# A transposed residual, weight DMAs alone on SyncE's queue, and a layernorm of more steps, in a recurrent attention kernel

## The chip, the cores and the metric

The kernel runs on one core of a Trainium2 chip. The metric is the device time of one execution in microseconds (us). The core has five engines that run their own instruction streams: TensorE (PE; its weight loads are listed as PEld), VectorE (DVE), ScalarE (ACT), GpSimd (POOL) and SyncE (SP). SyncE and ScalarE issue the DMAs of this kernel, each from its own stream and in its order (SPq and ACTq in the profile); the transfers run on 16 DMA engines that both share.

## The reference

`x` is 2048 tokens of 1024 features. `xn` is its layernorm. The result is `x + A(xn) + B(xn)`.

```python
def _A_ref(x, mem0, Wq, Wk, Wv, Wo, seg_len):
    mem = mem0
    for s in range(n_seg):
        xs = x[:, s * seg_len:(s + 1) * seg_len, :].copy()
        h = jnp.concatenate([mem, xs], axis=1)
        q = jnp.einsum('btd,dhe->bhte', h, Wq)
        k = jnp.einsum('btd,dhe->bhte', h, Wk)
        v = jnp.einsum('btd,dhe->bhte', h, Wv)
        scores = jnp.einsum('bhqe,bhke->bhqk', q, k) * scale
        ...
        o = jnp.einsum('bhqk,bhke->bhqe', p, v)
        o = jnp.einsum('bhte,hed->btd', o, Wo)
        mem = o[:, :M, :].copy()
        outs.append(o[:, M:, :])
    return jnp.concatenate(outs, axis=1)
```

A is attention with a memory: 64 segments of 32 tokens, each with 8 memory tokens in front, 32 heads of 128. The memory of a segment is the output of the segment before, so the segments follow one another. The four weights are 8 MB each in bfloat16. B scores all tokens with a vector `w_r`, takes the two best, sends them through a gated MLP of width 3584, scales the result by the sigmoid of the score and adds it to these two tokens; all others pass as they are. So the output is `x + xn` (with two rows changed), plus `xn` of B, plus attention; the kernel calls the first part the residual.

## The kernel before

**Weights.** The four attention weights are cut into 64 granules of 128 x 2048 (512 KB): numbers 0 to 47 are the six phases of Q, K and V (`PHASES`, two halves of each, 8 granules a phase), 48 to 63 are Wo. 42 granules stay on the chip (`wres`, loaded once by `load_resident`, lines 103 to 109); the other 22, spread evenly, are streamed again in every segment (`granule`, lines 319 to 324) through the four slots of the pool `wstream` (tiles named g). A load into a slot waits until TensorE has read what was in it, four streamed granules before.

**Prologue.** For 16 tiles of 128 tokens: load x (`load_x`), statistics (`ln_a`), normalise (`ln_b`), transpose on TensorE and score with w_r (`ln_c`), and write three things to DRAM (`ln_d`, lines 217 to 221): `xT_d`, the transposed xn by segment; `stl_d`, the last 8 tokens of each of four segments, transposed; and `xr_d`, x + xn, row by row. The loop of lines 227 to 236 runs these steps for neighbouring tiles; each step of VectorE, ScalarE and TensorE is issued in the program's order. `rounded` (lines 156 to 161) sends small values through bfloat16 and back with two copies. Then comes B (the MoE stage, lines 243 to 312): the two best tokens, 46 granules of its weights through the same four slots, and the two new rows written into `xr_d`.

**A segment** (lines 371 to 586). The 24 first tokens of the segment and the 8 memory tokens make 32 columns of ST, the stationary operand; a granule is the moving one, in four column groups of the array. The other 8 tokens of each segment ("left") fill the 32 columns of STL for four segments at once: with G, j = divmod(s, 4), left V is done in the segment j = 0 (tile PSl, line 493), left Q and K of the next group at j = 1 and 2 (written to DRAM by line 415 and read back as QL and KL), and left Wo at j = 3 (tile WL). After each Q or K phase ScalarE casts the sums (XB, line 500) and TensorE transposes them one granule later; `hook(p, kc, fn)` puts scores and attention behind given granules. Phase Wo (lines 523 to 563) starts from the residual: one matmul of an identity with RT, 24 rows of `xr_d` per 256 columns, and at j = 3 another with RL. At its end WO is cast to OB, written out by four DMAs of ScalarE (line 568), transposed and copied into the next ST (lines 352 to 357, the copy of line 356 is the hand-over to the next segment). At j = 3 some left Wo work follows, then OL is written out by sixteen DMAs of ScalarE (line 581).

**Order.** The schedule is manual: every engine gets its instructions in the order in which Python issues them. SyncE's queue holds all loads. Between the last granule of V and the first of Wo stand, for the next segment, QL and KL (line 347), ST (328), four RT (339), at j = 0 STL (333), and at j = 3 sixteen RL (532). SyncE runs ahead of TensorE as far as the four slots let it, and waits in place for whatever its next DMA needs. STL is one buffer and is loaded again when TensorE has finished left V. The DMAs of SyncE and ScalarE together take eight completion semaphores in turn, in the program's order; a DMA waits until the one eight before it has landed, whichever engine issued it.

Of the kernel before, what the change touches and what calls it, by code (L numbers as in the profile page):

```python
# [18 lines left out]
N_SLOT = 4  # L19
# [6 lines left out]
def kernel(  # L26
# [67 lines left out]
    xT_d = [dram.tile([4, P, KC * SEG], BF16, name=f"xT_d{t}") for t in range(NT)]  # L94
    stl_d = [dram.tile([P, KC * SEG], BF16, name=f"stl_d{t}") for t in range(NT)]
    ql_d = [dram.tile([2, P, 4, P], BF16, name=f"ql_d{t}") for t in range(NT)]
    kl_d = [dram.tile([2, P, 4, P], BF16, name=f"kl_d{t}") for t in range(NT)]
    xr_d = dram.tile([S, D], BF16, name="xr_d")
# [15 lines left out]
    RT = [const.tile([P, 256], BF16, name=f"RT{i}") for i in range(2)]  # L114
    PL = [const.tile([P, 4, 2, 32], BF16, name=f"PL{i}") for i in range(2)]
    for i in range(2):
        nc.gpsimd.memset(RT[i][:, :], 0.0)
        nc.gpsimd.memset(PL[i][:, :, :, :], 0.0)
# [10 lines left out]
    for jq in range(4):  # L129
        q0 = 32 * jq  # L130
        nc.gpsimd.affine_select(out=MF[q0:q0 + 32, 0:NK], in_=MF[q0:q0 + 32, 0:NK], pattern=[[-1, NK]],
                                compare_op=ALU.is_ge, fill=NEG, base=0, channel_multiplier=1)
        nc.gpsimd.affine_select(out=MF[q0:q0 + 32, NK:2 * NK], in_=MF[q0:q0 + 32, NK:2 * NK], pattern=[[-1, NK]],
                                compare_op=ALU.is_ge, fill=NEG, base=SEG, channel_multiplier=1)
    for jq in range(4):
        nc.vector.memset(MF[32 * jq:32 * jq + M, 0:NK], 0.0)
    nc.vector.tensor_copy(out=MASK[:, :], in_=MF[:, :])

    XT = {}
    XTS = []  # L140
    STS = []
    for i in range(2):
        XTS.append(pro1.tile([P, 4, KC, SEG], BF16, name=f"XTS{i}"))
        STS.append(pro1.tile([P, KC, 4, XL], BF16, name=f"STS{i}"))
        nc.gpsimd.memset(XTS[i][:, :, :, :], 0.0)
# [4 lines left out]
    I8 = const.tile([1, 8], U32, name="I8")  # L150

    def load_x(t):
        XT[t] = pro.tile([P, D], BF16, tag="XT", bufs=3, name="XT")
        nc.sync.dma_start(out=XT[t][:, :], in_=x2[t * P:(t + 1) * P, :])

    def rounded(pool, ap, shape, tag):
        tb = pool.tile(shape, BF16, tag=tag + "b", name=tag + "b")
# [26 lines left out]

    stats = {}
    pend = {}

    def ln_a(t):
        stats[t] = ln_stats(pro, XT[t], P)

# [33 lines left out]
    if NT > 1:  # L224
        load_x(1)
# [394 lines left out]
```

## Time and profile before

| what | us |
|---|---|
| median of 3 runs (lowest, highest) | 3179.71 (3167.09, 3187.45) |
| the profiled execution, its own time | 3181.84 |
| its span, first to last instruction | 3180.1 |
| first segment's hand-over | 248.6 |
| mean granted TensorE clock, share of full | 0.836 |

How to read the lines: a row of the page's groups has line, engine, operation, output <- inputs and count, then busy time and mean of one in ns, then the idle time ahead of them and what ended it. "A <- B" in the waits means that engine and line A stood idle until B was done: total us, times, longest. A window's row gives the stretch and its length, busy time and count for each engine, granted clock, share of the 16 DMA engines' time, and GB/s moved.

### The profile page before, as it was taken

How to read it: one execution, taken by the hardware profiler on the slowest of the kernel's cores; microseconds unless marked ns; L12 is line 12 of the kernel's file. 1: busy time of each engine (PE TensorE's matmuls, PEld its weight loads, DVE VectorE, ACT ScalarE, POOL GpSimd, SP SyncE). 2: the span in 40 equal slices, each digit the busy share in tenths (PEclk: the TensorE clock that was granted, in tenths of full speed). 3: DMA queues.
4: the chain of work that ended last, by engine and by line, in shares of the span. 5: the costliest groups of instructions: out<-in, count | busy, mean ns of one | idle time of the engine just before them, and what ended most of it. 6: DMA issues, size and time to landing. Idle time of an engine off the chain costs nothing.

```text
span 3180.1 us, 81705 instructions
## 1 busy us (share of the span) xinstructions
PE 2005.7 (63%) x36305; PEld 1010.8 (32%) x36305; DVE 737.7 (23%) x2158; ACT 447.1 (14%) x1001; POOL 87.9 (3%) x292
## 2 busy tenths in 40 slices
PE   2245656677676756666676666766676666757566
PEld 1122323333333333333333333333333333323333
DVE  4301212122122212212221222212221221222122
ACT  2201111111111111111111111111111111111111
POOL 2200000000000000000000000000000000000000
PEclk9997988878778888888788888778788888888887
DMA  6685878878687877878687787868787787868787
GB/s 208 209 307 176 302 251 277 271 240 280 234 282 244 279 267 250 277 259 299 224 284 269 265 273 250 300 225 280 257 282 264 237 285 258 292 231 286 264 282 241
DMA packets 366682, 831.69 MB, mean 262 GB/s; under 512 B 73428, under 2 KB 118516, under 8 KB 366328
## 3 DMA queue, kind: packets, MB, share of 16 engines
q1 hardware_dynamic: 343800, 813.86, 75.8%
q10 hardware_dynamic: 22528, 12.61, 1.3%
q8 instruction: 284, 4.65, 0.6%
q14 instruction: 70, 0.57, 0.1%
HBM read 804.28 MB, written 22.02 MB: 260 GB/s over the span
## 4 chain that ended last, share of the span: by engine, by line
DMA 57%; PE 25%; DVE 6%; SPq 4%; issue 2%; ACT 2%; ACTq 0%; POOL 0%; DVEq 0%; POOLq 0%
DMA g<-in_A_Wo_dram 16%; DMA g<-in_A_Wq_dram 16%; DMA g<-in_A_Wv_dram 11%; PE PSm L489 10%; DMA g<-in_A_Wk_dram 7%; PE WO L540 6%; PE PSl L493 3%; SPq L532 2%; DMA out_dram<-OB 2%; PE PTq L396 1%; DMA kl_d<-QS 1%; PE WL L540 1%; DMA QL<-ql_d 1%; DVE SPS L438 1%; DVE NM L437 1%
## 5 line engine op out<-in xcount | busy, mean ns | idle before, releaser
L489 PE MATMUL PSm<-wres,ST 128*32 128x512 bf16 x8192 | 789.7, 428 | 15.5 <-DVE ST L356 14.3
L489 PE MATMUL PSm<-g,ST 128*32 128x512 bf16 x4096 | 451.7, 428 | 362.8 <-DMA g<-in_A_Wq_dram 176.1
L489 PEld LDWEIGHTS <-ST 128*32 128x32 bf16 x12288 | 330.5, 101 | 815.5 <-issue 499.8
L540 PEld LDWEIGHTS <-OT 128*32 128x32 bf16 x8192 | 260.4, 117 | 335.4 <-issue 286.0
L540 PE MATMUL WO<-g,OT 128*32 128x256 bf16 x3072 | 203.9, 354 | 243.8 <-DMA g<-in_A_Wo_dram 242.9
L540 PE MATMUL WO<-wres,OT 128*32 128x256 bf16 x5120 | 302.6, 350 | 0.0
L500 ACT CAST XB<-PSm 128x512 bf16<-128x512 f32 x256 | 149.5, 584 | 784.0 <-PE PSm L489 477.3
L493 PE MATMUL PSl<-wres,STL 128*32 128x512 bf16 x2048 | 221.7, 418 | 49.6 <-DVE VL L513 48.3
L475 DVE CAST OTL<-OP 128x64 bf16<-128x64 f32 x256 | 57.5, 225 | 729.8 <-ACT OT L473 729.8
L396 PE MATMUL PTq<-IDENT,XB 128*128 128x128 bf16 x1024 | 112.0, 238 | 163.9 <-ACT XB L500 161.8
L473 ACT CAST OT<-OP 128x256 bf16<-128x256 f32 x256 | 95.2, 372 | 820.5 <-PE OP L470 820.5
L396 PEld LDWEIGHTS <-XB 128*128 128x128 bf16 x1024 | 63.7, 104 | 292.6 <-ACT XB L500 265.3
L401 DVE COPY QT<-PTq 128x512 bf16<-128x512 bf16 x128 | 52.4, 409 | 387.2 <-PE PTq L396 387.2
L437 DVE TENSOR_REDUCE NM<-SPS 128x8 f32<-128x320 f32 x128 | 62.9, 492 | 311.4 <-PE SPS L432 311.4
L493 PEld LDWEIGHTS <-STL 128*32 128x32 bf16 x3072 | 92.0, 103 | 130.7 <-issue 85.2
L440 ACT ACTIVATE EX<-SPS 128x320 bf16<-128x320 f32 x128 | 55.9, 437 | 540.6 <-DVE SPS L438 516.5
L404 DVE COPY KT<-PTq 128x512 bf16<-128x512 bf16 x128 | 54.4, 425 | 329.1 <-PE PTq L396 327.1
L468 PE MATMUL OP<-PTM,VM 32*128 32x40 bf16 x2048 | 105.4, 192 | 33.1 <-DVE VM L510 32.4
L468 PEld LDWEIGHTS <-VM 32*128 32x128 bf16 x2048 | 73.3, 99 | 146.1 <-issue 107.3
L422 POOL COPY KT<-KL 128x128 bf16<-128x128 bf16 x128 | 37.4, 292 | 2947.9 <-PE SPS L429 1933.5
L493 PE MATMUL PSl<-g,STL 128*32 128x512 bf16 x1024 | 112.5, 423 | 6.1 <-DVE XBl L504 6.1
L470 PE MATMUL OP<-PTL,VL 32*128 32x40 bf16 x2048 | 101.6, 188 | 0.0
(103 smaller groups left out, 1511.8 us busy)
## 6 DMA issues: line engine op xcount, KB each, us to landing
g<-in_A_Wq_dram SPq DMA_DIRECT2D x384, 512.0 KB
g<-in_A_Wo_dram SPq DMA_DIRECT2D x384, 512.0 KB
g<-in_A_Wk_dram SPq DMA_DIRECT2D x320, 512.0 KB
g<-in_A_Wv_dram SPq DMA_DIRECT2D x320, 512.0 KB
mg<-in_B_w_gate_dram SPq DMA_DIRECT2D x16, 448.0 KB
mg<-in_B_w_up_dram SPq DMA_DIRECT2D x16, 448.0 KB
mg<-in_B_w_down_dram SPq DMA_DIRECT2D x14, 512.0 KB
wres<-in_A_Wk_dram SPq DMA_DIRECT2D x11, 512.0 KB
```

The costliest lines, as they stand in the source:

```text
L396: nc.tensor.transpose(out=PTq[:, il, :, :].rearrange("p j r -> p (j r)"), in_=XB[:, il * P:(il + 1) * P], identity=IDENT[:, :])
L437: nc.vector.tensor_reduce(out=NM[:, :], in_=S8, axis=AX.X, op=ALU.max, negate=True)
L440: nc.scalar.activation(out=EX[:, :, :], in_=S8, func=ACTF.Exp, scale=SCALE)
L468: nc.tensor.matmul(o, lhsT=VM[q0:q0 + 32, c0:c0 + P], rhs=PTm[q0:q0 + 32, il, 0:NK], start=True, stop=False, tile_position=(q0, 0), skip_g ...
L470: nc.tensor.matmul(o, lhsT=VL[q0:q0 + 32, c0:c0 + P], rhs=PTl[q0:q0 + 32, il, 0:NK], start=False, stop=True, tile_position=(q0, 0), skip_g ...
L473: nc.scalar.copy(out=OT[half][:, 2 * ph:2 * ph + 2, :, :], in_=ov[:, :, :, 0:SEG])
L475: nc.vector.tensor_copy(out=OTL[:, h0:h0 + 8, j, :].rearrange("p (a i) r -> p a i r", a=2), in_=ov[:, :, :, SEG:NK])
L489: nc.tensor.matmul(PSm[32 * jq:32 * jq + 32, :], lhsT=ST[:, kc, :], rhs=Gv[:, 512 * jq:512 * (jq + 1)], start=(kc == 0), stop=(kc == KC - ...
L493: nc.tensor.matmul(PSl[32 * jq:32 * jq + 32, :], lhsT=STL[:, kc, :], rhs=Gv[:, 512 * jq:512 * (jq + 1)], start=(kc == 0), stop=(kc == KC - 1),
L500: nc.scalar.copy(out=XB[:, :], in_=PSm[:, :])
L532: nc.sync.dma_start(out=RL[32 * g + XL * sg:32 * g + XL * (sg + 1), :], in_=xr_d[t0:t0 + XL, 256 * g:256 * (g + 1)])
L540: nc.tensor.matmul(PS[32 * g:32 * g + 32, 0:256], lhsT=lhs(h), rhs=Gv[:, D * hs + 256 * g:D * hs + 256 * (g + 1)], start=False, stop=(last ...
```

## The change

1. **Layernorm of more steps.** The copies of `rounded` go: the small tiles are bfloat16 themselves. The loop runs 20 iterations instead of 18, with statistics of tile t, normalisation of t - 1, transposes of t - 2, scores of t - 3 and writes of t - 4. x is loaded by pairs of tiles into slots of `wstream`. TensorE transposes x + xn as well as xn (16 transposes a tile instead of 8), and `zT_d`, the transposed x + xn by segment, replaces `xr_d`.
2. **Residual by TensorE.** `fetch_z` loads ZT, the segment's part of `zT_d` (64 KB, one DMA); GpSimd saves its last 8 tokens into ZL and clears them in ZT. `residual` adds ZT by eight matmuls with the identity (at j = 3 eight more with ZL). RT, RL and their 4 and 16 loads go. The two rows of B are transposed and written into `zT_d` element by element.
3. **Queues.** `fetch` issues the next streamed granule when one has been used, in a list `flow` that runs through the MoE stage and all segments without a break; SyncE issues nothing else in the segments. ScalarE issues ZT behind granule (1, 4), ST behind (2, 3), QKL (QL and KL in one tile and one DMA) behind the second scores, and STL after the phases.
4. **Output.** The memory tokens stand last of the 32 and no longer first; the mask follows. OL is written by four DMAs instead of sixteen.

The core of the diff:

```diff
-    def load_r(s):
-        R = RT[s % 2]
-        for g in range(4):
-            nc.sync.dma_start(out=R[32 * g + M:32 * g + SEG, :], in_=xr_d[s * SEG:s * SEG + XM, 256 * g:256 * (g + 1)])
+    flow = [("gu", w, kc, fh) for w in range(2) for kc in range(KC) for fh in range(2)]
+    flow += [("dn", fg) for fg in range(FC // 2)]
+    flow += [("w", g) for s in range(NSEG) for g in sorted(streamed)]
...
+    def fetch():
+        if not flow:
+            return
+        what = flow.pop(0)
+        t = wstream.tile([P, 2048], BF16, tag="g", name="g")
...
+    def used(g):
+        if g in streamed:
+            fetch()
...
+    def residual(PS, Zt):
+        for g in range(4):
+            for c in range(2):
+                nc.tensor.matmul(PS[32 * g:32 * g + 32, c * P:(c + 1) * P], lhsT=Zt[:, 2 * g + c, :], rhs=IDENT[:, :],
+                                 start=(c == 0), stop=False, tile_position=(0, 32 * g), skip_group_check=True)
...
+        def fetch_z():
+            Zt = nxt["z"] = one.tile([P, KC, SEG], BF16, tag="zt", name="ZT")
+            nc.scalar.dma_start(out=Zt[:, :, :], in_=zT_d[s])
+            nc.gpsimd.tensor_copy(out=ZL[:, :, j, :], in_=Zt[:, :, XM:SEG])
+            nc.gpsimd.memset(Zt[:, :, XM:SEG], 0.0)
...
+        hook(1, 4, fetch_z)
+        hook(2, 3, fetch_st)
...
-        if s + 1 < NSEG:
-            qkl_n = load_ql(s + 1)
-            ST_n = load_st(s + 1)
-            load_r(s + 1)
-            if j == 0 and G + 1 < NT:
-                STL = load_stl(G + 1)
+        if j == 0 and G + 1 < NT:
+            STL = load_stl(G + 1)
         WO = psA.tile([P, 512], F32, tag="acc", name="WO")
-        nc.tensor.matmul(WO[:, 0:256], lhsT=IDENT[:, :], rhs=RT[s % 2][:, :], start=True, stop=False, skip_group_check=True)
+        residual(WO, nxt["z"])
...
             for g in range(4):
-                for sg in range(4):
-                    t0 = (4 * G + sg) * SEG + XM
-                    nc.scalar.dma_start(out=out2[t0:t0 + XL, 256 * g:256 * (g + 1)],
-                                        in_=OL[32 * g + XL * sg:32 * g + XL * (sg + 1), :])
+                nc.scalar.dma_start(out=o4[:, XM:SEG, 256 * g:256 * (g + 1)], in_=OL[32 * g:32 * (g + 1), :])
```

Three places in the engines' order follow. First SyncE's queue around the Wo phase of a segment j = 3 (the numbers behind a name count buffers and DRAM tensors), before:

```order
L323 DMA g<-in_A_Wv_dram 128x2048 x5
L347 DMA QL<-ql_d_124 128x2x128
L347 DMA KL<-kl_d_140 128x2x128
L328 DMA ST<-xT_d_92 128x256
L339 DMA RT_154<-xr_d 24x256 x4
L532 DMA RL<-xr_d 8x256 x16
L323 DMA g<-in_A_Wo_dram 128x2x1024 x6
L323 DMA g<-in_A_Wq_dram 128x2048 x3
```

and with the change:

```order
L248 DMA g<-in_A_Wv_dram 128x2048 x5
L248 DMA g<-in_A_Wo_dram 128x2x1024 x6
L248 DMA g<-in_A_Wq_dram 128x2048 x3
L248 DMA g<-in_A_Wk_dram 128x2048 x2
L248 DMA g<-in_A_Wq_dram 128x2048 x3
```

The 23 loads between the granules of Wv and of Wo are gone from this queue.

Second ScalarE from the end of a segment j = 3 into the segment j = 0 behind it, before:

```order
L565 CAST OB<-WO 128x128
L568 DMA out_dram<-OB 24x256 x4
L577 CAST OL<-WL 128x256
L581 DMA out_dram<-OL 8x256 x16
L500 CAST XB<-PSm 128x512 x2
L440 ACTIVATE EX<-SPS 128x320
L500 CAST XB<-PSm 128x512 x2
L440 ACTIVATE EX<-SPS 128x320
L509 CAST VM<-PSm 128x256
```

and with the change:

```order
L571 CAST OB<-WO 128x128
L574 DMA out_dram<-OB 24x256 x4
L583 CAST OL<-WL 128x256
L586 DMA out_dram<-OL 4x8x256 x4
L517 CAST XB<-PSm 128x512
L397 DMA ZT<-zT_d 128x256
L517 CAST XB<-PSm 128x512
L336 DMA ST<-xT_d_88 128x256
L451 ACTIVATE EX<-SPS 128x320
L517 CAST XB<-PSm 128x512 x2
L451 ACTIVATE EX<-SPS 128x320
L347 DMA QKL<-qkl_d_121 128x4x128
```

Twelve of the writes of OL are gone, and three loads stand between the casts and the exponents.

Third VectorE in the layernorm loop (sd, ve, ri are columns of 128 values, DX is x minus its mean), the second half of one tile before:

```order
L158 CAST verb<-ve 128x1
L160 CAST verf<-verb 128x1
L158 CAST sdrb<-sd 128x1
L160 CAST sdrf<-sdrb 128x1
L181 RECIPROCAL ri<-sdrf 128x1
L182 TENSOR_SCALAR DX<-XT,mvrf 128x1024
L206 COPY STS_205<-PTx 128x256
L214 CAST RROW<-PR 1x4x24
L215 CAST RROW<-PR 1x4x8
```

and one iteration with the change:

```order
L153 BN_STATS s_333<-XP 128x6 x2
L155 BN_AGGR mv<-s_333 128x2
L157 TENSOR_SCALAR ve<-mv 128x1
L164 RECIPROCAL ri<-sd 128x1
L165 TENSOR_SCALAR Z<-XP,mv 128x1024
L183 COPY Tz<-PTx 128x8x4x32
```

The copies between the small tiles and both casts of RROW are gone from VectorE, a copy of 128 x 1024 takes the place of one of 128 x 256, and the rows of one iteration belong to three tiles.

More of the change, by code (lines that the diff above doesn't have):

```diff
@@ L94 @@
     xT_d = [dram.tile([4, P, KC * SEG], BF16, name=f"xT_d{t}") for t in range(NT)]
+    zT_d = dram.tile([NSEG + 1, P, KC, SEG], BF16, name="zT_d")
     stl_d = [dram.tile([P, KC * SEG], BF16, name=f"stl_d{t}") for t in range(NT)]
-    ql_d = [dram.tile([2, P, 4, P], BF16, name=f"ql_d{t}") for t in range(NT)]
-    kl_d = [dram.tile([2, P, 4, P], BF16, name=f"kl_d{t}") for t in range(NT)]
-    xr_d = dram.tile([S, D], BF16, name="xr_d")
+    qkl_d = [dram.tile([2, 2, P, 4, P], BF16, name=f"qkl_d{t}") for t in range(NT)]
     res_tiles = {}
```

286 lines of the change are left out of this document (137 added, 149 removed).

## The prediction

> **What bounds the kernel now.** I read the head of the page first, then the busy time by windows, then the timeline of SyncE's queue inside the windows that stand out, and the table of waits last, to see how often each of them comes.
>
> ```profile
> span 3180.1 us, 81705 instructions
> PE 2005.7 (63%) x36305; PEld 1010.8 (32%) x36305; DVE 737.7 (23%) x2158; ACT 447.1 (14%) x1001; POOL 87.9 (3%) x292
> q1 hardware_dynamic: 343800, 813.86, 75.8%
> DMA 57%; PE 25%; DVE 6%; SPq 4%; issue 2%; ACT 2%; ACTq 0%; POOL 0%; DVEq 0%; POOLq 0%
> L356 DVE COPY ST<-PTm x64: 191/192/193, 248.6 to 3126.5; 128x64 bf16<-128x64 bf16 x64
> ```
>
> The chain that ended last is 57% DMA, yet the 16 DMA engines are busy 75.8% of the span on that queue. No engine is near full. The copy of line 356 ends each segment's hand-over, so the first segment starts at 248.6 us, and a group of four takes (3126.5 - 248.6) / 63 x 4 = 182.7 us. Here is one group (segments 32 to 35) by window; the columns are the stretch and its length, busy time of PE, PEld, DVE, ACT and POOL, then granted clock, DMA share and GB/s.
>
> ```profile
> 1724.40:1777.30 52.90, 32.33 (x581) 16.03 (x573) 10.23 (x31) 6.42 (x16) 0.76 (x4) 0.77 0.67 222
> 1777.30:1819.60 42.30, 29.85 (x541) 14.89 (x541) 10.79 (x30) 6.67 (x15) 0.76 (x4) 0.84 0.85 283
> 1819.60:1860.70 41.10, 28.69 (x541) 14.22 (x541) 10.95 (x31) 6.67 (x15) 0.76 (x4) 0.92 0.90 299
> 1860.70:1907.20 46.50, 30.46 (x554) 15.31 (x558) 9.52 (x28) 5.60 (x13) 0.82 (x4) 0.74 0.77 258
> ```
>
> Length times rate gives 11.7, 12.0, 12.3 and 12.0 MB: every segment moves the same 12 MB, 48.0 MB a group, and the long segments are those with a low rate. Cutting the same group where the rate falls shows that the loss sits in five places:
>
> ```profile
> 1726.00:1740.00 14.00, 5.14 (x64) 2.03 (x60) 0.42 (x1) 0.96 (x2) 0.00 (x0) 0.68 0.48 157
> 1740.00:1755.00 15.00, 11.42 (x214) 4.94 (x207) 5.47 (x14) 2.96 (x7) 0.38 (x2) 0.95 0.94 313
> 1755.00:1765.00 10.00, 5.89 (x93) 2.42 (x93) 3.38 (x12) 1.50 (x5) 0.38 (x2) 0.83 0.10 22
> 1765.00:1805.00 40.00, 27.90 (x492) 14.21 (x493) 9.58 (x27) 5.55 (x12) 0.38 (x2) 0.83 0.90 299
> 1805.00:1808.00 3.00, 2.78 (x56) 1.17 (x53) 0.83 (x4) 0.80 (x3) 0.38 (x2) 0.71 0.47 98
> 1808.00:1845.00 37.00, 25.42 (x485) 13.07 (x485) 8.37 (x22) 5.76 (x13) 0.38 (x2) 0.88 0.95 317
> 1845.00:1849.00 4.00, 2.36 (x38) 0.88 (x39) 2.34 (x8) 0.48 (x2) 0.38 (x2) 0.78 0.42 93
> 1849.00:1887.00 38.00, 25.55 (x441) 11.82 (x439) 8.43 (x25) 5.23 (x12) 0.38 (x2) 0.81 0.91 309
> 1887.00:1895.00 8.00, 3.75 (x57) 1.27 (x53) 1.76 (x6) 1.12 (x3) 0.44 (x2) 0.50 0.13 23
> 1895.00:1907.00 12.00, 9.31 (x243) 7.15 (x243) 0.74 (x3) 1.01 (x3) 0.00 (x0) 0.71 0.95 336
> ```
>
> In the five long stretches (15, 40, 37, 38 and 12 us) the stream runs at 299 to 336 GB/s, 44.2 MB in 142 us or 311 GB/s, with DMA shares of 0.90 to 0.95: there the kernel is bound by its weights, and PE has a quarter to a third of the time free. In the five short ones (39 us) it moves 3.3 MB. What SyncE's queue does then:
>
> ```profile
> 1752.77 0.38 SPq L347 DMA_DIRECT2D QL<-ql_d  x1
> 1753.20 0.46 SPq L347 DMA_DIRECT2D KL<-kl_d  x1
> 1753.71 0.47 SPq L328 DMA_DIRECT2D ST<-xT_d  x1
> 1754.21 2.54 SPq L339 DMA_DIRECT2D RT<-xr_d  x4
> 1763.02 0.36 SPq L333 DMA_DIRECT2D STL<-stl_d  x1
> 1763.42 7.01 SPq L323 DMA_DIRECT2D g<-in_A_Wo_dram  x6
> ...
> 1885.21 2.12 SPq L339 DMA_DIRECT2D RT<-xr_d  x4
> 1888.07 5.59 SPq L532 DMA_DIRECT2D RL<-xr_d  x16
> 1893.70 6.84 SPq L323 DMA_DIRECT2D g<-in_A_Wo_dram  x6
> ```
>
> The queue is in order. From 1752.8 on it issues small loads; at 1756.8 it reaches the load of STL, whose tile TensorE still reads, and stands until 1763.0, and the six granules of Wo stand behind it. At j = 3 the sixteen RL loads take their place. No weight is requested for some 9 us, the four slots run empty, and TensorE waits for the refill. The remaining stall, 1726 to 1740, is ScalarE's:
>
> ```profile
> 1726.47 0.37 ACT L577 CAST OL<-WL 128x256 bf16<-128x256 f32 x1 [2.91 <-DMA g<-in_A_Wk_dram]
> 1726.87 9.41 ACTq L581 DMA_DIRECT2D out_dram<-OL  x16
> 1736.33 0.58 ACT L500 CAST XB<-PSm 128x512 bf16<-128x512 f32 x1 [9.48 <-DMA out_dram<-OL]
> ```
>
> Sixteen small writes hold ScalarE for 9.41 us; the cast of the first Q phase stands behind them, TensorE's transposes wait for the cast, and no weight slot comes free.
>
> **The change, part by part.** *The five stalls.* At 311 GB/s the 3.27 MB of the short stretches would take 10.5 us of their 39, so they lose 6.9 (OL), 9.3 (STL), 2.0, 2.8 (QL to RT) and 7.4 (RL): 28.5 us a group. The change takes every non-weight load out of SyncE's queue, so four of the five go whole. The OL writes become 4 instead of 16; at 9.41 / 16 = 0.59 us each, 2.35 us stay. I count 28.5 - 2.35 = 26.1 us a group, 418 us over 16 groups. This account is by bytes: it holds if TensorE can do the work it did in the stalls during the quiet stretches. The other end is that it cannot: then only the time that PE was idle in the short stretches comes back, (14 - 5.14) + (10 - 5.89) + (3 - 2.78) + (4 - 2.36) + (8 - 3.75) = 19.1, less 2.35, 16.7 us a group or 268 us. I take the first, since TensorE is free for 11.6 of 37 and 12.1 of 40 us in the quiet stretches.
>
> A rule of the Trainium skill speaks against this part: the page "DMA: Bandwidth & Descriptors", section "Issuing engines are not separate DMA queues", has it that issuing from more engines saves only the sequencer's time to start the DMA, as they all run on the same 16 engines. By that rule the moved loads would give their issue times alone; with 0.38 + 0.46 + 0.47 + 2.12 a segment, 5.59 and 0.36 a group and the 4.6 of OL that is 24.3 us a group, 389 us in all and an end at 2760. By the row below the wait, not the issue, is the larger share at STL, so I keep 418.
>
> ```profile
> SPq L333 <- PE PSl L493: 102.1, 15, 8.4
> PE WO L540 <- DMA g<-in_A_Wo_dram: 242.9, 181, 5.0
> ```
>
> *What ScalarE takes over.* ZT, ST and QKL each segment, STL each group: some 0.46 us each by the rows of KL and ST, 1.4 us a segment on an engine busy 6 of 45. ZT and ST stand just behind a cast of XB and the next cast is a phase later; QKL stands behind the exponent of the second scores. STL stands behind the copies of VL, which already wait for what it waits for. Behind a blocked load stand the casts of XB and the copies of OT, and TensorE waits for both. Cost 0; with that cover gone 1.4 x 64 = 90 us. GpSimd copies ZL and clears part of ZT before the KT copy of scores(0); it is busy 0.76 us a segment, and only a late ZT would delay the scores.
>
> *Residual.* Eight matmuls of 128 columns (sixteen at j = 3) replace one of 256. Eight transposes of that size took 1.05 us in the prologue (row below), so at most 1.05 x 80 = 84 us; they stand where TensorE now waits for Wo, 242.9 us in 181 times, so at least 0. I take 10, nearer to the covered end.
>
> *Prologue.* Columns as above, then three rows of timeline and chain:
>
> ```profile
> 0.00:162.00 162.00, 35.43 (x385) 26.93 (x385) 65.26 (x252) 38.42 (x52) 38.92 (x36) 1.00 0.67 212
> 176.00:242.00 66.00, 32.83 (x480) 18.74 (x477) 1.19 (x3) 0.22 (x1) 0.00 (x0) 0.97 0.89 307
> 242.00:250.00 8.00, 1.42 (x10) 0.47 (x11) 2.13 (x4) 0.00 (x0) 0.00 (x0) 0.56 0.09 26
> ```
>
> ```profile
> 66.73 0.33 SPq L154 DMA_DIRECT2D XT<-in_A_x_dram  x1
> 75.53 0.33 SPq L154 DMA_DIRECT2D XT<-in_A_x_dram  x1
> ```
>
> ```profile
> 127.15 1.05 PE PTx L202 x8
> ```
>
> A layernorm tile takes 8.8 us (75.53 - 66.73) though VectorE, the busiest, needs 65.26 / 16 = 4.1: it is one serial chain. Spread over four iterations, it is bound by its bytes: 212 x 162 = 34.3 MB, about the same after the change (zT_d for xr_d). At the 307 GB/s of the MoE stage that is 112 us, a gain of 50. The bounds are 50 and 0; I take 38, since the loads of x still wait for buffers that GpSimd frees, one iteration behind. At 242 to 250 the queue is empty; the change has four granules fetched by then, 2.1 MB or 6.8 us, of which the transposes and element-wise write of ZNEW take some back: 3 us.
>
> *Sum.* 3180.1 - 418 - 38 - 3 + 10 = 2731 us of span. The profiled execution itself took 3181.84, 0.07% above the median of 3179.71, so I give 2730. A segment would then take (182.8 - 26.1) / 4 = 39.2 us at 48.0 / 156.7 = 306 GB/s.
>
> **The rivals.** *TensorE becomes the bound* (chance 0.25): the lower account, 268 for 418: 2881. For it: at j = 0 PE is busy 5.89 of the 10 us of the STL stall, work that stays. Against it: its free third in the quiet stretches.
>
> *The stream gets faster* (0.12): without the stalls it runs throughout as in the last row of the cuts, 336 GB/s: 48.0 / 0.336 = 142.9 us a group, 39.9 saved, 638 in all: 2511. For it: the granted clock is 0.50 in the RL stall and 0.95 at 1740 to 1755, so less waiting gives a faster PE and earlier free slots. Against it: 299 to 317 in the other four stretches, and 0.81 at 1849 to 1887 with no stall inside. The Trainium skill ("TensorE: Matmul & The Clock Gate", Part 1) says the gate halves the clock after an idle window of about 3.4 us and opens after a busy one; these two clocks agree, though 0.83 in the STL stall shows that idle DMA is not idle PE.
>
> *ScalarE inherits the waiting* (0.03): its DMAs share eight completion semaphores with SyncE's and each waits for the eighth DMA before it. If one load a segment is held as long as the OL writes hold the cast now, 9.48 us, that is 64 x 9.48 = 607 us: 3338, slower. It decides from (418 + 38 + 3 - 10) / 64 = 7.0 us a segment. Against it: in the program's order the weight DMA eight before such a load is one that TensorE has mostly used already.
>
> *The change doesn't do what it says* (0.02): SyncE is held by its eight semaphores whenever a ScalarE DMA is late, the stalls stay, and only the prologue pays: 3180 - 38 - 3 + 10 = 3149.
>
> **How the numbers follow.** My forecast has 0.58, the rivals 0.25, 0.12, 0.03 and 0.02. Its own span is 2671 (all 28.5 us, prologue 50, no residual cost) to 2807 (halfway to the lower account, 21.4 us a group). For 8 in 10 the range takes in the TensorE case at 2881 and reaches down toward 2511 until about a tenth is left out: 2590 to 2890. About 1% is what a measurement of this kernel tells from no change: faster by more 0.95, within it 0.02, slower 0.03.
>
> **What would show it.** In the new profile SyncE's issues should be weights alone from the first segment on, and its waits for PSl and the RL row gone; windows of one segment should read 36 to 42 us with DMA shares of 0.88 or more, j = 0 at most 4 us above the others; ScalarE's wait for OL should fall below 3 us a group; the first matmul of the MoE stage should come before 142 us. I am wrong if ScalarE's casts wait for DMAs more than now, if a DMA share below 0.5 stays in any 8 us, or if PE is busy over 90% of the segments.

## The result, and the profile after

| | before | after |
|---|---|---|
| median of the runs on one chip (lowest, highest), us | 3180.24 (3167.09, 3187.45) | 2812.60 (2806.56, 2824.20) |
| span of the profiled execution, us | 3180.1 | 2810.0 |
| mean granted TensorE clock | 0.836 | 0.864 |

The ratio is 0.8852, with a 95% interval of 0.8812 to 0.8893: 368 us less, where the prediction had 450 less. The time lies inside its range and 83 us above its 2730. This is the head of the page of the kernel after; the fourth line is the chain that ended last.

```profile
span 2810.0 us, 82148 instructions
PE 1949.7 (69%) x36873; PEld 998.7 (36%) x36873; DVE 722.0 (26%) x2021; ACT 459.1 (16%) x1017; POOL 112.9 (4%) x436
q1 hardware_dynamic: 292212, 796.00, 82.7%
DMA 47%; PE 22%; issue 19%; DVE 7%; ACT 2%; ACTq 1%; POOL 1%; SPq 1%; POOLq 0%; DVEq 0%
```

The weights still bound it, but the queue's share of the DMA engines' time is 82.7% where 75.8% stood. The hand-over copy, from the busy time by line:

```profile
L355 DVE COPY ST<-PTm x64: 191/192/193, 200.3 to 2764.5; 128x64 bf16<-128x64 bf16 x64
```

Set against the same row of before (248.6 to 3126.5), the 370.1 us between the two spans split into three: the first segment starts 48.3 us earlier, the 63 steps between hand-overs take 2564.2 us in place of 2877.9, which is 313.7 less, and the last segment takes 45.5 in place of 53.6, which is 8.1. A group of four takes 162.8 us where it took 182.7. From the starts of the hand-over copies of segments 8 to 59, the mean of a segment went from 53.9, 42.3, 41.5 and 44.9 us (j = 0 to 3) to 42.6, 42.4, 38.2 and 37.9: j = 0 gave 11.3 us, j = 3 7.0, j = 2 3.3 and j = 1 nothing.

Windows of one group after (segments 32 to 35, columns as in the prediction), and two cuts inside the first two:

```profile
1513.60:1556.70 43.10, 29.22 (x588) 15.01 (x580) 10.17 (x30) 6.53 (x16) 1.08 (x6) 0.88 0.81 285
1556.70:1601.20 44.50, 31.73 (x548) 15.43 (x548) 10.95 (x30) 6.77 (x15) 1.08 (x6) 0.81 0.80 264
1601.20:1637.90 36.70, 27.09 (x548) 14.20 (x548) 10.92 (x30) 6.77 (x15) 1.08 (x6) 0.95 0.95 328
1637.90:1678.00 40.10, 28.42 (x568) 14.68 (x572) 9.54 (x29) 5.60 (x13) 1.08 (x6) 0.83 0.91 304
1540.00:1547.00 7.00, 6.57 (x92) 2.53 (x95) 0.83 (x4) 0.74 (x2) 0.00 (x0) 0.54 0.42 130
1572.00:1578.50 6.50, 4.00 (x65) 1.52 (x64) 2.83 (x8) 0.91 (x2) 1.08 (x6) 0.74 0.46 169
```

j = 2 and 3 are as forecast. j = 0 and 1 each keep one stall, at 130 and 169 GB/s. SyncE's timeline (start and length in us, queue, line, operation, output <- input, count) in the third segment of the group shows weights alone:

```profile
1604.51 2.48 SPq L248 DMA_DIRECT2D g<-in_A_Wq_dram  x3
1607.96 4.72 SPq L248 DMA_DIRECT2D g<-in_A_Wk_dram  x3
1613.62 6.75 SPq L248 DMA_DIRECT2D g<-in_A_Wv_dram  x5
1621.58 9.89 SPq L248 DMA_DIRECT2D g<-in_A_Wo_dram  x6
```

And the rows of the waits that bear on the two stalls (total us, times, longest):

```profile
ACT XB L517 <- DMA out_dram<-OL: 56.9, 15, 4.6
PE SPS L438 <- POOL KT L434: 52.4, 17, 5.7
PE PSl L509 <- DVE VL L530: 47.0, 16, 3.1
```

The wait for OL is a third of what it was (158.6 us in 15 times before). TensorE's wait for KT comes 17 times, about once a group, where it was 6.2 us in 2 times before. The wait for VL is old: 48.3 us in 16 times before.

**The stall of j = 1.** Rows of the timeline of all engines, 1564 to 1575 us:

```profile
1564.78 0.66 ACTq L397 DMA_DIRECT2D ZT<-zT_d  x1
...
1573.40 0.24 POOL L398 COPY ZL<-ZT 128x64 bf16<-128x64 bf16 x1 [44.92 <-DMA ZT<-zT_d]
...
1573.78 0.29 POOL L434 COPY KT<-QKL 128x128 bf16<-128x128 bf16 x1
...
1574.12 0.23 PE L438 MATMUL SPS<-KT,QT 128*32 128x40 bf16 x4 [2.52 <-POOL KT L434]
```

ScalarE reaches ZT's load 8.1 us into the segment, behind a cast, the copy QS and the write of left Q. The 64 KB land 8.6 us after that, among granules of 512 KB. (Over segments 8 to 59 the load is issued 8.1 us into a segment with j = 1 and GpSimd's copy starts 7.8 us after the issue; at the other j these are 3.8 to 5.8 and 5.4 to 5.6 us.) GpSimd stands at the copy of ZL until then, the KT copy stands behind it, and TensorE's scores behind the KT copy. While TensorE stands it frees no slot.

**The stall of j = 0**, likewise:

```profile
1539.33 0.40 DVE L466 STREAM_TRANSPOSE PTL<-PL 128x256 bf16<-128x256 bf16 x1
1539.66 0.39 DVE L527 CAST VM<-PSm 128x256 bf16<-128x256 f32 x1
1539.97 0.41 DVE L530 CAST VL<-PSl 128x256 bf16<-128x256 f32 x1
1540.43 0.62 PE L509 MATMUL PSl<-wres,STL 128*32 128x512 bf16 x4 [3.15 <-DVE VL L530]
```

VectorE's half of VL stands behind the softmax of the second scores, while ScalarE's half was cast at 1538.03. TensorE waits 3.15 us for the buffer PSl and then runs at half speed: its groups of four matmuls start every 0.43 us until 1546.1, and every 0.22 us after that.

The prologue by windows: the layernorm, the MoE stage, the hand-over. The stream is close to full in the first and the second, and the third is long.

```profile
0.00:114.00 114.00, 44.86 (x385) 37.03 (x385) 50.80 (x120) 44.11 (x68) 43.44 (x52) 0.88 0.97 316
122.00:188.00 66.00, 32.79 (x504) 19.16 (x502) 1.39 (x3) 0.73 (x2) 0.00 (x0) 0.63 0.94 321
188.00:200.30 12.30, 0.72 (x10) 0.40 (x10) 2.61 (x5) 0.00 (x0) 0.00 (x0) 0.64 0.41 108
```

### The profile page after: what moved, and what is told of

It reads as the page before. It is cut to its first block, busy times and chain, and to the rows that moved or that the text cites. A ratio compares the mean times of both kernels' runs of the same rounds, so it can differ in the third digit from the quotient of the medians.

```text
span 2810.0 us, 82148 instructions
## 1 busy us (share of the span) xinstructions
PE 1949.7 (69%) x36873; PEld 998.7 (36%) x36873; DVE 722.0 (26%) x2021; ACT 459.1 (16%) x1017; POOL 112.9 (4%) x436
## 3 DMA queue, kind: packets, MB, share of 16 engines
q1 hardware_dynamic: 292212, 796.00, 82.7%
## 4 chain that ended last, share of the span: by engine, by line
DMA 47%; PE 22%; issue 19%; DVE 7%; ACT 2%; ACTq 1%; POOL 1%; SPq 1%; POOLq 0%; DVEq 0%
DMA g<-in_A_Wq_dram 14%; DMA g<-in_A_Wo_dram 13%; PE PSm L505 10%; DMA g<-in_A_Wv_dram 7%; DMA g<-in_A_Wk_dram 5%; PE WO L545 4%; DMA out_dram<-OB 2%; PE PSl L509 2%; DMA zT_d<-Tz 1%; PE PTq L408 1%; DMA qkl_d<-QS 1%; DVE SPS L449 1%; DVE NM L448 1%; ACT EX L451 1%; DVE DN L453 1%
## 5 line engine op out<-in xcount | busy, mean ns | idle before, releaser
L505 PE MATMUL PSm<-wres,ST 128*32 128x512 bf16 x8192 | 806.3, 436 | 14.7 <-DVE ST L355 13.9
L545 PEld LDWEIGHTS <-OT 128*32 128x32 bf16 x8192 | 233.7, 107 | 178.9 <-issue 153.6
L509 PE MATMUL PSl<-wres,STL 128*32 128x512 bf16 x2048 | 233.5, 443 | 50.3 <-DVE VL L530 47.0
L545 PE MATMUL WO<-g,OT 128*32 128x256 bf16 x3072 | 178.0, 313 | 121.6 <-DMA g<-in_A_Wo_dram 120.4
L545 PE MATMUL WO<-wres,OT 128*32 128x256 bf16 x5120 | 254.3, 305 | 0.0
L408 PEld LDWEIGHTS <-XB 128*128 128x128 bf16 x1024 | 61.8, 102 | 203.0 <-ACT XB L517 172.2
L481 PE MATMUL OP<-PTM,VM 32*128 32x40 bf16 x2048 | 102.0, 186 | 42.5 <-DVE VM L527 38.2
L398 POOL COPY ZL<-ZT 128x64 bf16<-128x64 bf16 x64 | 15.1, 236 | 2424.7 <-DMA ZT<-zT_d 2246.7
```

The costliest lines, as they stand in the source:

```text
L408: nc.tensor.transpose(out=PTq[:, il, :, :].rearrange("p j r -> p (j r)"), in_=XB[:, il * P:(il + 1) * P], identity=IDENT[:, :])
L481: nc.tensor.matmul(o, lhsT=VM[q0:q0 + 32, c0:c0 + P], rhs=PTm[q0:q0 + 32, il, 0:NK], start=True, stop=False, tile_position=(q0, 0), skip_g ...
L505: nc.tensor.matmul(PSm[32 * jq:32 * jq + 32, :], lhsT=ST[:, kc, :], rhs=Gv[:, 512 * jq:512 * (jq + 1)], start=(kc == 0), stop=(kc == KC - ...
L509: nc.tensor.matmul(PSl[32 * jq:32 * jq + 32, :], lhsT=STL[:, kc, :], rhs=Gv[:, 512 * jq:512 * (jq + 1)], start=(kc == 0), stop=(kc == KC - 1),
L545: nc.tensor.matmul(PS[32 * g:32 * g + 32, 0:256], lhsT=lhs(h), rhs=Gv[:, D * hs + 256 * g:D * hs + 256 * (g + 1)], start=False, stop=(last ...
```

## The experiments

Each ratio is to the kernel before on the same chip, with its 95% interval. The first seven ask what caused the stalls that went, the next four what caused those that stayed, the last is on the prologue.

**1. The OL writes alone.** In the kernel before, the sixteen writes of OL become four:

```diff
+            o4 = out2[4 * G * SEG:4 * (G + 1) * SEG, :].rearrange("(s r) d -> s r d", s=4)
             for g in range(4):
-                for sg in range(4):
-                    t0 = (4 * G + sg) * SEG + XM
-                    nc.scalar.dma_start(out=out2[t0:t0 + XL, 256 * g:256 * (g + 1)],
-                                        in_=OL[32 * g + XL * sg:32 * g + XL * (sg + 1), :])
+                nc.scalar.dma_start(out=o4[:, XM:SEG, 256 * g:256 * (g + 1)], in_=OL[32 * g:32 * (g + 1), :])
```

> The kernel before, with the left-over rows written by 4 DMAs in place of 16, and nothing else. The account by bytes (16 writes hold ScalarE for 9.41 us, 12 x 0.59 = 7.1 us fewer, of which 4.55 are lost stream time at 311 GB/s): 16 x 4.55 = 73 us, 3107 us; all of the 7.1 would be 113 us, 3067. Rival (the stream at the start of j = 0 waits for something else as well, such as the reload of the slots): under 25 us, 3155 us or more.

Measured 3074.26 us, 0.9681 (0.9654 to 0.9707): 105 us less, between the two amounts that the first theory named (73 and 113) and near the upper. ScalarE's timeline at a group's end:

```profile
1673.46 3.61 ACTq L580 DMA_DIRECT2D out_dram<-OL  x4
1677.11 0.59 ACT L500 CAST XB<-PSm 128x512 bf16<-128x512 f32 x1 [3.68 <-DMA out_dram<-OL]
```

The cast is held 3.68 us here, no longer 9.48. By the waits the hold falls from 158.6 to 60.0 us in 15 times, 6.6 us a time, and the mean of j = 0 falls by 6.9 us, from 53.9 to 46.9. So the hold counts in full, and not only its bytes.

**2. The order alone.** In the kernel before, each granule is asked for right behind the use of the one whose slot it takes; all loads stay on SyncE at their places.

```diff
     def granule(g):
...
-        t = wstream.tile([P, 2048], BF16, tag="g", name="g")
-        nc.sync.dma_start(out=granule_out(t, g), in_=granule_dram(g))
+        got, t = queued.pop(0)
...
         return t
+
+    def used(g):
+        if g in streamed:
+            fetch()
...
+                used(8 * p + kc)
```

> The kernel before with the order of the weight DMAs alone taken from the change: each granule is asked for right after the one whose slot it takes was used, four ahead, still on SyncE; QL, KL, ST, RT, STL and RL stay on SyncE, at their old places, and OL keeps its 16 writes. Theory (order): a load that waits no longer has a weight behind it whose slot was free, so of the 21.5 us a group lost at SyncE most come back; four granules in flight cover some 6.8 us, and at j = 3 the loads take 9.4 us to issue, so 2 to 3 us stay there: 3180 less 16 x 15 to 19, 2875 to 2940 us, and SyncE's wait for PSl at STL becomes harmless. Rival (engine): as long as the small loads share SyncE's queue the stalls stay, over 3100 us.

Measured 3186.43 us, 1.0025 (0.9999 to 1.0050): nothing. The theory is refuted; the rival's number came, though run 3 takes its reason away. TensorE's timeline at j = 3:

```profile
1899.59 0.39 PE L552 MATMUL WL<-RL,IDENT 128*128 128x256 bf16 x1 [9.85 <-DMA RL<-xr_d]
1899.91 0.62 PE L558 MATMUL WO<-g,OT 128*32 128x256 bf16 x8
```

The Wo granules are there now, but TensorE's own stream is in order too. It comes to the residual's matmul and stands 9.85 us until RL has landed, 154.7 us in 16 times by the waits. In the kernel before it was 61.8 us in 16 times, and behind this wait came one for a granule: the two ran side by side.

```profile
1895.25 0.37 PE L534 MATMUL WL<-RL,IDENT 128*128 128x256 bf16 x1 [3.90 <-DMA RL<-xr_d]
1897.77 0.62 PE L540 MATMUL WO<-g,OT 128*32 128x256 bf16 x8 [2.15 <-DMA g<-in_A_Wo_dram]
```

The other segments have no such wait for RL. There the stall moves. Four granules are asked for ahead of the small loads now, but the next one still stands behind them, and TensorE waits for that one. From the timelines of SyncE and TensorE at j = 0 of run 2 (QL, KL and ST, from 1764.35 on, stand ahead of the first row):

```profile
1765.88 1.61 SPq L354 DMA_DIRECT2D RT<-xr_d  x4
1767.91 0.36 SPq L348 DMA_DIRECT2D STL<-stl_d  x1
1768.36 1.59 SPq L327 DMA_DIRECT2D g<-in_A_Wo_dram  x2
...
1772.23 0.62 PE L558 MATMUL WO<-g,OT 128*32 128x256 bf16 x8 [3.15 <-DMA g<-in_A_Wo_dram]
```

**3. The engine alone.** In the kernel before, QL, KL, ST, RT, STL and RL are issued by ScalarE at their old places. One of five calls:

```diff
-        nc.sync.dma_start(out=STL.rearrange("p k r -> p (k r)"), in_=stl_d[g][:, :])
+        nc.scalar.dma_start(out=STL.rearrange("p k r -> p (k r)"), in_=stl_d[g][:, :])
```

> The kernel before with the engine alone changed: QL, KL, ST, RT, STL and RL are issued by ScalarE at their old places, behind the fifth phase, and SyncE issues weights alone in its old order. Theory (either is enough, since a queue of weights alone is in order by itself): the four stalls of SyncE go here too, 16 x 15 to 21 us, but the 16 RL loads now hold ScalarE for 5.6 us a group in front of the OT copies, so 2840 to 2980 us. Rival (ScalarE inherits the waiting, the prediction's third rival): the OT copies stand behind STL's and RL's loads, TensorE waits for them, and the time stays above 3050 us.

Measured 3173.45 us, 0.9988 (0.9958 to 1.0017): nothing. The wait for RL is 159.8 us in 16 times, and at j = 0 ScalarE's timeline has what the prediction's third rival describes:

```profile
1764.95 4.01 ACTq L339 DMA_DIRECT2D RT<-xr_d  x4
1770.41 0.36 ACTq L333 DMA_DIRECT2D STL<-stl_d  x1
1770.82 0.37 ACT L473 CAST OT<-OP 128x256 bf16<-128x256 f32 x1 [6.96 <-DMA RT<-xr_d]
```

A copy of OT stands 6.96 us behind the loads of RT: ScalarE has taken the stand over from SyncE. The Trainium skill ("DMA: Bandwidth & Descriptors", section "Issuing engines are not separate DMA queues") has it that issuing from more engines saves only the time that a sequencer takes to issue. By that rule the engine is worth little, and the runs agree with it and not with the reason that the prediction gave against it.

**4. The place alone.** In the kernel before, still on SyncE in the old order, the next ST and RT are loaded at (2, 3), RL at (1, 4) of j = 3:

```diff
+        if j == 3:
+            hook(1, 4, early_rl)
+        hook(2, 3, early_st)
...
-            ST_n = load_st(s + 1)
-            load_r(s + 1)
+            ST_n = nxt["st"]
```

> The kernel before with the place alone changed: the loads of the next ST and RT stand at the hook (2,3) of the segment before, and the 16 loads of RL at (1,4) of j = 3, all still on SyncE and in single loads; QL, KL and STL stay behind the fifth phase, the weights in their old order. Theory (a dependence, not a queue: TensorE's in-order stream comes to the residual's matmul right behind the fifth phase and stands there until RL, or RT, has landed, whoever issued it and whatever weights are in flight): j = 3 falls from 44.9 to 38 to 40 us and j = 1, 2 by 1 to 2 us, 16 x 7 to 11, 3005 to 3070 us. Rival (SyncE's issue time: 16 + 4 loads stand in front of weights in any place): within 1% of before.

Measured 3134.95 us, 0.9869 (0.9847 to 0.9891): 45 us less, under half of the least that was expected, so neither theory holds alone. The wait for RL is gone, but j = 3 keeps its length, 45.1 us; the gain lies at j = 1 and 2, whose means fall by 2.4 and 1.6 us. SyncE's timeline at its start:

```profile
1835.36 0.33 SPq L323 DMA_DIRECT2D g<-in_A_Wk_dram  x1
1836.19 8.99 SPq L485 DMA_DIRECT2D RL<-xr_d  x16
1845.27 0.35 SPq L323 DMA_DIRECT2D g<-in_A_Wk_dram  x1
```

The sixteen loads now hold up Wk for 8.99 us in place of Wo. Each load takes 0.29 us to issue, as it did at the old place; the rest of the 8.99 us stands between the first three of them. The operand is early; the weights behind it are late.

**5. Place and OL together.** Edits 1 and 4 in one kernel.

> The kernel before with the place as in the run beside it and OL written by 4 DMAs: two of the stalls cured, SyncE's queue as it was. If the gains add (OL alone gave 105), this is 105 us below the run beside it, 2900 to 2965 us, and the rest to the changed kernel is its prologue (48 us) and STL. Rival (the stalls hide one another): less than half of the 105.

Measured 3066.52 us, 0.9663 (0.9633 to 0.9694): 68 us below run 4, of 105. More than half, less than the sum; the gains overlap. Seen from run 1 the place adds nothing that can be told: 0.9663 for 0.9681, and the intervals overlap.

**6. The engine given back.** In the changed kernel, ST, STL, QKL and ZT are issued by SyncE, at their new places and in the new order. One of four calls:

```diff
-            nc.scalar.dma_start(out=Zt[:, :, :], in_=zT_d[s])
+            nc.sync.dma_start(out=Zt[:, :, :], in_=zT_d[s])
```

> The changed kernel, with the loads of ST, STL, QKL and ZT issued by SyncE again, at the places in the program where ScalarE issues them now, so that the order stays (weights one slot ahead, asked for right after the granule that frees the slot was used) and the engine goes back. Theory of the prediction (the stalls went because the small loads left SyncE's queue): the stand at STL, 6.2 us a group, and the issue time of three loads a segment, 1.4 us, come back: 16 x (6.2 + 5.6) = 189 us, about 3000, at least 2900. Rival (the order removed the stalls: what a load waits for, TensorE being done with a tile, comes no later than the slot of the next weight, so a waiting load delays no weight): within 1.5% of 2812.6, 2790 to 2855 us.

Measured 2786.11 us, 0.8761 (0.8743 to 0.8780): 26 us less than the changed kernel. The prediction's reason had demanded at least 2900. SyncE at the new place of QKL:

```profile
1569.87 1.26 SPq L347 DMA_DIRECT2D QKL<-qkl_d  x1
1571.22 7.09 SPq L248 DMA_DIRECT2D g<-in_A_Wo_dram  x4
```

The granule behind the load is held little: TensorE is through with its slot at 1570.59, and it is asked for at 1571.22. The gain is at j = 1, 40.3 us in place of 42.4, and 0.5 at j = 0; j = 2 and 3 lose 0.8 and 0.7. ZT's load is issued earlier at j = 1, 7.3 us into the segment on the mean where it was 8.1 (5.7 in this segment). Run 11 bears on this.

**7. Engine and order given back.** As run 6, and in the segments each granule is asked for just before its use, as in the kernel before:

```diff
     def granule(g):
-        return take("w", g) if g in streamed else res_tiles[g]
+        if g not in streamed:
+            return res_tiles[g]
+        if not queued:
+            fetch()
+        return take("w", g)
     def used(g):
-        if g in streamed:
-            fetch()
+        pass
```

> The changed kernel with both the engine and the order as before: ST, STL, QKL and ZT on SyncE, and in the segments each granule asked for just before its use in the program, so that a waiting load has weights behind it; places and residual stay as changed. Theory (place and residual alone made the gain): within 1.5% of the 2786 us that the loads on SyncE with the new order took. Rival (with the loads at their new places the order does count: QKL's load waits for the second scores and STL's for the fifth phase, weights behind them): 2 to 4 us in each of 64 segments and 4 in each group, 2970 us or more.

Measured 3071.30 us, 0.9664 (0.9648 to 0.9680): 285 us more than run 6, so here the order counts. SyncE in one segment with j = 2:

```profile
1747.34 1.80 SPq L248 DMA_DIRECT2D g<-in_A_Wv_dram  x2
1756.31 0.38 SPq L350 DMA_DIRECT2D QKL<-qkl_d  x1
1756.74 1.51 SPq L248 DMA_DIRECT2D g<-in_A_Wv_dram  x3
```

From 1749.1 to 1756.3 the queue stands at QKL, whose tile the second scores still read, and three granules of Wv stand behind it. The waits of SyncE have 418.0 us in 63 times for this, and 152.6 us in 15 times at the load of STL. In the window 1753.5 to 1757:

```profile
1753.50:1757.00 3.50, 2.97 (x65) 1.50 (x65) 1.41 (x3) 0.69 (x2) 0.00 (x0) 1.00 0.14 51
```

What follows from runs 2, 3, 4, 6 and 7: whoever takes away one wait meets the next. At j = 3 two ran side by side: weights stood behind the loads of RL in an in-order queue, and TensorE stood before its residual for what these loads bring. In the other segments the small loads, left at their place, hold the next granule (run 2) or ScalarE's copies (run 3). Alone, the order gives nothing, the engine nothing and the place 45 us. In the changed kernel, with fewer and earlier loads on SyncE, the order is worth 285. Part of that may lie at QKL's new place: SyncE stands there 418.0 us in 63 times, and stood at the load of QL in the kernel before 135.5 us in 63.

Three things were not run: place and order together in the kernel before, the old order with ScalarE's loads in the changed kernel, and the change with the old number of loads. So the runs show that the loads needn't go to ScalarE once the order is new. Whether ScalarE would do in place of the new order, and what the fewer loads and the residual's new form give by themselves, stays open.

**8. ZL later.** In the changed kernel GpSimd's copy of ZL and its clearing of ZT move from (1, 4) to (3, 0), behind the KT copy of the first scores; the load stays.

```diff
             nc.scalar.dma_start(out=Zt[:, :, :], in_=zT_d[s])
+        def split_z():
+            Zt = nxt["z"]
             nc.gpsimd.tensor_copy(out=ZL[:, :, j, :], in_=Zt[:, :, XM:SEG])
             nc.gpsimd.memset(Zt[:, :, XM:SEG], 0.0)
...
+        hook(3, 0, split_z)
```

> The changed kernel, with GpSimd's copy of ZL and clearing of ZT moved from the hook at (1,4) to (3,0), behind the KT copy of the first scores; the ZT load stays. Theory (the late ZT): at j = 1 the load lands some 9 us after its issue, GpSimd's in-order queue stands there, the KT copy behind it and TensorE's scores behind that (2.5 us of PE wait, then a slow clock and 5 us without a weight request). Then j = 1 falls from 42.4 to about 39 us, 3 to 4 us in each of 16 segments: 2750 to 2765 us, and PE's wait for the KT copy (52.4 us in 17) nearly goes. Rival (j = 1 is long because of its left Q and K projections, and the stream only moves its gap): j = 1 stays above 41.5 and the time within 1% of 2812.6.

Measured 2752.17 us, 0.8655 (0.8637 to 0.8673): 60 us less, the theory's number. j = 1 falls to 39.5 us, j = 0 stays at 43.0, and TensorE's wait for KT is 9.0 us in 2 times.

**9. VL by ScalarE alone**, ahead of its half of VM:

```diff
                 c0 = half * 512
+                if PSl is not None:
+                    nc.scalar.copy(out=VL[:, c0:c0 + 512], in_=PSl[:, :])
                 nc.scalar.copy(out=VM[:, c0:c0 + 256], in_=PSm[:, 0:256])
                 nc.vector.tensor_copy(out=VM[:, c0 + 256:c0 + 512], in_=PSm[:, 256:512])
-                if PSl is not None:
-                    nc.scalar.copy(out=VL[:, c0:c0 + 256], in_=PSl[:, 0:256])
-                    nc.vector.tensor_copy(out=VL[:, c0 + 256:c0 + 512], in_=PSl[:, 256:512])
```

> The changed kernel, with both halves of VL copied by ScalarE, ahead of its half of VM, in place of one half by each of ScalarE and VectorE. Theory (VectorE's half of VL stands behind the softmax of the second scores at j = 0, TensorE's next V phase waits 3.1 us for the buffer, 16 times, and then runs at a low clock in which no slot comes free): the wait falls to under 1.5 us and j = 0 from 42.6 to 39 to 41 us, 16 x 1.6 to 3.5: 2755 to 2787 us. Rival (the stretch is bound by TensorE's main and left V matmuls, whatever the copy does): the wait shrinks, j = 0 keeps its length to 0.5 us and the time stays within 1% of 2812.6.

Measured 2748.43 us, 0.8637 (0.8610 to 0.8663): 64 us less, a little more than the theory's range allowed. From the waits, and the window of segment 32:

```profile
PE PSl L509 <- ACT VL L527: 15.8, 16, 1.1
```

```profile
1487.90:1527.50 39.60, 26.52 (x588) 14.20 (x588) 9.54 (x28) 6.95 (x16) 1.08 (x6) 1.00 0.88 293
```

The wait falls from 47.0 to 15.8 us in all, 2 us a time, but j = 0 falls by 2.9, to 39.7. The rest fits the clock: in the changed kernel groups every 0.43 us follow this wait in all 16 segments with j = 0, and here they follow none of the waits of 1.0 to 1.1 us. The granted clock is 1.00 in this segment where 0.88 stood; the mean of j = 0 goes from 0.88 to 0.92. That the clock makes all of the 0.9 us is argued, not shown.

**10. Both cures together.**

> The changed kernel with both cures together: ZL's copy behind the first scores, VL copied by ScalarE alone. If the two stalls are apart, the gains of 60 and 64 us add up: 2685 to 2700 us, j = 0 and j = 1 both under 40 us, a group of four at about 155 us, which is the 26 us a group that the prediction had put on the stalls. Rival (they share one reserve, or the stream takes the freed time back): under two thirds of the sum, 2730 us or more.

Measured 2709.27 us, 0.8529 (0.8491 to 0.8567): 103 us less than the changed kernel, of 125. It falls between the two expectations, nearer to the sum, and it is faster than both kernels of the case. Segments 32 to 35:

```profile
1463.70:1503.60 39.90, 27.36 (x588) 14.49 (x585) 9.55 (x29) 6.96 (x16) 1.16 (x6) 0.96 0.91 309
1503.60:1543.20 39.60, 28.45 (x548) 14.05 (x548) 10.94 (x30) 6.79 (x15) 1.09 (x6) 0.91 0.90 292
1543.20:1582.40 39.20, 27.98 (x548) 14.37 (x548) 10.93 (x30) 6.78 (x15) 1.15 (x6) 0.91 0.93 311
1582.40:1621.70 39.30, 26.96 (x568) 14.26 (x572) 9.55 (x29) 5.61 (x13) 1.15 (x6) 0.87 0.89 310
```

Four equal segments, and the mean of all steps between hand-overs (198.8 to 2658.5) is 39.0 us.

**11. Both cures and the loads on SyncE**, runs 6 and 10 together.

> The changed kernel with both cures (ZL's copy behind the first scores, VL by ScalarE alone) and with the loads of ST, STL, QKL and ZT on SyncE, in the new order. The loads on SyncE gave 26 us by an earlier ZT. Theory (that gain is the late ZT's, which the moved copy already has): within 0.7% of 2709, 2690 to 2728 us. Rival (it is a gain of its own, ScalarE being freed of 1.4 us of issue a segment): 2695 us or less.

Measured 2710.22 us, 0.8522 (0.8500 to 0.8543), the same as run 10. So the 26 us of run 6 were the late ZT's, and for the rest it makes no difference in this order which engine issues the loads.

**12. The layernorm of the old depth.** In the changed kernel's loop, normalisation, transposes and scores of a tile stand in one iteration and its writes in the next:

```diff
-    for t in range(NT + 4):
+    for t in range(NT + 2):
...
-        if 0 <= t - 4:
-            ln_e(t - 4)
+        if 0 <= t - 2:
+            ln_e(t - 2)
...
-        if 0 <= t - 2 < NT:
-            ln_c(t - 2)
-        if 0 <= t - 3 < NT:
-            ln_d(t - 3)
+        if 0 <= t - 1 < NT:
+            ln_c(t - 1)
+            ln_d(t - 1)
```

> The changed kernel with its layernorm loop in the old depth: a tile's normalization, transposes and router product in one iteration, its writes one later, in place of four iterations; the merged steps, tiles loaded in pairs and the second set of transposes stay. Theory (depth made the prologue's gain of 48 us): 30 to 50 us come back, 2842 to 2863. Rival (fewer VectorE steps and paired loads made it): under 15 us, 2828 or less.

Measured 2824.92 us, 0.8872 (0.8836 to 0.8909). Against the changed kernel's 0.8852 (0.8812 to 0.8893) the intervals overlap, so the total, 12 us by the medians and the rival's number, doesn't settle it. The stage does: the first segment's hand-over stands at 222.2 us, 21.9 later than in the changed kernel, and the window of the layernorm reads

```profile
0.00:136.00 136.00, 48.31 (x385) 36.30 (x385) 48.77 (x120) 45.94 (x68) 43.24 (x52) 1.00 0.84 262
```

where the deeper loop moves the same bytes at 316 GB/s. Depth made about 22 of the prologue's 48 us; the other 26 lie in the edits that stayed, which no run took apart.

## Why the prediction was right, and where it was wrong

**Right: what bounds the kernel, and by how much it could gain.** The account by bytes gave a segment 39.2 us at 306 GB/s once nothing stalls the stream. Run 10, without the two stalls that were left, has 39.0 us, and its four windows move 48.3 MB in 158.0 us, 305 GB/s. TensorE was not the bound: at 69% of the span it takes the work of the stalls.

That the time lies in the range is in part luck. The cause below was wrong, and the change brought the order, the place and the fewer loads along with the engine that the prediction relied on.

**Wrong: "The change takes every non-weight load out of SyncE's queue, so four of the five go whole."** This is the step that failed, in its cause and in its size. With every such load out of SyncE's queue and nothing else changed, the time stays as it was (run 3), and with the new order the loads may stand in that queue again (run 6). The order of the weights, the place of the loads and what TensorE itself waits for decide it. The prediction read SyncE's row of sixteen RL loads and the missing weights behind them, and passed over TensorE's own stand before WL. The residual, which it costed as eight small matmuls, took that wait away: even at j = 1, where it is late, ZT lands 17 us before its matmuls (1573.40 and 1590.45), and RL's sixteen loads are gone.

**Mis-sized: the sum of the stalls.** 418 us were forecast from all five; 322 came, the 313.7 and 8.1 above, with the residual's cost inside. OL, put at (6.9 - 2.35) x 16 = 73 us, gave 105 alone, since the hold counts whole. Its 0.59 us a write was no issue time: one of the sixteen takes 0.31 us (the median of line 581), one of the four 0.63 (line 580 of run 1), and the rest of the 9.41 and 3.61 us stands between the writes; by the waits 3.8 us stay, not 2.35. If OL gave as much in the change as alone, which run 5 puts in doubt, the other four gave 217 of 345. Most of the difference has two names. "Only a late ZT would delay the scores" named its own condition and costed it at nothing; ZT was late at j = 1 and cost 60 us (run 8). And the window of 10 us at j = 0, booked whole to the load of STL, held a second wait, which this change doesn't touch and which costs 64 us (run 9). In the kernel before:

```profile
1757.29 0.40 PE L493 MATMUL PSl<-wres,STL 128*32 128x512 bf16 x4 [3.15 <-DVE VL L513]
```

This is left V, whose end the load of STL awaits until 1763.0, so the wait for VL lengthened that stand too. Both cures together give 103 us, more than the 83 that the forecast missed by. OL and the prologue gave 32 and 7 us more than forecast; some 25 us of the 345 remain, of which the forecast allowed 10 for the residual, and no run takes the rest apart.

**ScalarE inherits the waiting** came true in run 3, behind RT. In the change the casts of XB wait less for output writes than before, 137 us in place of 290.

**Prologue.** Its bytes at the stream's rate were the right bound: they allowed a gain of 50 us, and the first matmul of the MoE stage came 53.3 us earlier (121.9 for 175.2), with a DMA share of 0.97 up to 114 us. The hedge, 38 of 50, was not needed; the MoE stage itself ends 53.5 us earlier (187.8 for 241.3). The hand-over lost what was to be gained by prefetching: 12.5 us for 7.3, since in the chain the first write of ZNEW holds the second for 4.08 us, and the last load of OB behind them takes another 2.79. So 48.3 in place of 41.

**Residual.** Ten us were allowed. Eight matmuls of ZT take 0.43 us (1590.45, x8), the one of RT took 0.39; over 80 of them that is 3 us.

**What was to show it.** SyncE's weights alone, the first MoE matmul at 121.9 and TensorE's share came out. Windows of 36 to 42 us with a DMA share of 0.88 did so at j = 2 and 3 only; j = 0 lies 4.4 to 4.6 above them, and the wait for OL is 3.8 us a time where under 3 was said. One sign of being wrong came too, a DMA share below 0.5 in 8 us: it is 0.47 from 1540 to 1548 us and 0.44 from 1573.5 to 1581.5, at the two stalls that stayed.

## What to carry to other kernels

When an engine and a DMA queue stand still at the same time, list what each of them would wait for next before booking the stall to one: here the queue's order and its engine were worth nothing alone and the operand's place 45 us, while the order was worth 285 once the loads were fewer and early. A load that may wait did little harm in a queue of weights where the weights ahead of it filled every slot and it was one short load (run 6); seven or more of them still held the next granule (run 2). A step "costed at nothing unless it is late" needs the time of its load: issue plus landing, counted from the place in the program where its engine really gets there.

## What the runs showed of the hardware

- A wait of TensorE of 3.15 us was followed by 5.7 us at half speed (groups every 0.43 us for 0.22). Such groups followed this wait in all 16 segments with j = 0 of the changed kernel, three times after only 2.0 to 2.1 us, and none of the waits of 1.0 to 1.1 us in run 9. The Trainium skill ("TensorE: Matmul & The Clock Gate", Part 1) gives an idle window of about 3.4 us as what halves the clock. The trace agrees only roughly, since 3.15 us is a little and 2.0 us well under that.
- A load of 64 KB took 8.6 us to land among granules of 512 KB.
- One write of OL took ScalarE 0.31 us to issue in sixteen pieces and 0.63 in four (medians), so a quarter of the writes halves the issue time. The holds, 9.41 and 3.6 us, are longer, since the writes also stand between one another.
- Sixteen loads of RL took SyncE 8.99 us at the start of a segment (run 4) and 5.59 at its end in the kernel before. One load takes 0.29 us at both places (medians); the difference is waiting between the loads.
